# Half-block products for a first wave, a third half-block group for the second, and one written order for both

## The chip, the cores and the metric

The kernel runs on one core of a Trainium2 chip. The metric is the device time of one execution in microseconds (us). The core's engines are TensorE (PE in the profile, its weight loads PEld), VectorE (DVE), ScalarE (ACT), GpSimd (POOL) and SyncE (SP, which here issues most DMAs). Each works through its own queue in order and waits on semaphores for the others.

## The reference, cut to what matters

Block-wise linear attention with a decay `lam` for each head, over 4 batches, 8 heads, 768 positions of 64 values, in blocks of 64 with a carried state; then a two-layer MLP on the 3072 tokens of 512 values, with a quick gelu and a hidden width of 2048:

```python
for b in range(nb):
    intra = np.einsum('bhic,bhjc->bhij', qb, kb) * Dmask[None]
    intra = np.einsum('bhij,bhjd->bhid', intra, vb)
    inter = np.einsum('bhid,bhde->bhie', qb * lam_pow[None], kv_state)
    out[:, :, sl] = intra + inter
    kv_state = lam_block[None, :, None, None] * kv_state + np.einsum('bhsd,bhse->bhde', kb_dec, vb)

h = x @ w_in                                # 3072x512 @ 512x2048
g = h * (1.0 / (1.0 + np.exp(-1.702 * h)))
return (g @ w_out).astype(np.float32)       # 3072x2048 @ 2048x512
```

The kernel computes in bf16 with f32 sums and writes f32.

## The kernel before

**Waves.** The 3072 tokens are worked through in six waves of 512. Waves 0 and 1 (`w < ND`) take the first 256 positions of two batches each, `c` naming the batch of the pair; waves 2 to 5 take 128 positions of all four batches. While TensorE does the MLP of one wave, the attention of the next is put between its products. All of it stands under a manual schedule: the order of the instructions in the source is the order in each engine's queue, and the framework adds the semaphores.

**Attention of waves 0 and 1.** `do_cast` multiplies k or q by powers of `lam` and casts to bf16 (line 202, four operations of 128x256 a tile, on VectorE or GpSimd, with two SBUF inputs). `turn_pe` transposes on TensorE and copies out of PSUM on ScalarE. `cast_v` casts v. `d_scores` makes the scores of two pairs of heads and masks them on VectorE (line 267). `d_one` and `d_state` make the state, `d_keep` copies it to SBUF on ScalarE, `d_even` and `d_inter` read that copy. `d_out` makes the output; `d_x` copies it to `xT`, the MLP's input, one half by ScalarE and one by ScalarE or VectorE. For waves 2 to 5 the casts (line 209, GpSimd, eight instructions a wave) are followed by DMA transposes; a one-element copy on GpSimd (`gate_pool`, line 655) holds these casts back until the last of the wave's `x_sums`.

**Products by parts of the sum.** Most of the MLP is done by a scheme that forms a 2x2 block product from seven block products in place of eight. Its operands are blocks and sums of blocks, made on VectorE: `in_sums(g)` for `w_in` (tiles `w_in_t`, line 519, per group `g` of four 128-column blocks), `x_sums(w)` for the tokens (`x_s`, line 528), `weight_sums(j)` for chunk `j` of `w_out` (`w_out_t`, line 426) and `g_sums` for the hidden layer (`g_s`, line 439). The products are numbered 1 to 7 and gathered in three PSUM banks: X takes 1, then 6, 5 and 3 on top of it, Q takes 2, V takes 7 and then 4. Results leave between them: 1, 6 and 7 are copied out as `part` (ScalarE, or VectorE where the step ends in `v`), 2, 5 and 4 are `part` plus the bank (VectorE, lines 551 and 483), 3 is the bank itself. So product 6 has to wait for the copy of 1, 5 for that of 6, 3 for the sum of 5, and 4 for the copy of 7.

**First MLP product.** `in_product(w, g, n, ...)` is product `n` of group `g` for 256 of the 512 tokens by two output blocks: 4 matmuls of 256 columns. `mlp1` (line 402) and `mlp1_half` (line 414) are the plain forms, with 512 and 256 columns; their results go through gelu on ScalarE to `g_sb`. In wave 0 everything is plain; in wave 1 two groups (`GR[1]` = 0 and 3) are done by parts and the eight other blocks by `mlp1_half`; from wave 2 on all four groups are done by parts.

**Second MLP product.** `product(w, n, ts)` does product `n` for a wave (line 459). Wave 0 alone uses the plain `mlp2` (line 571): four groups of 128 tokens, 16 matmuls of 512 columns each.

**The order.** For waves 0 and 1 the order comes from a list of products (`main`) with the other work hung in at fractional places (`side`); from wave 1's groups on it is the string `STEPS[w]`, read by `one_step`. There a letter `a` to `d` with a digit is product n of the first to the fourth group, the capital with a digit its gelu, `Pnt` product n of the second MLP product for token half t, `S`, `M`, `m`, `R` parts of the next wave's attention, `X` its `x_sums`, `gl` and `gh` the `g_sums`, `K`, `Q`, `k`, `q` casts, `G` the gate, and `+` a step of the next wave.

**PSUM.** Eight banks in two rings: `mm` with three and `a` with five (`acc`). A new tile takes a bank of its ring and waits for the last reader of what stood there.

**DMA.** `w_in` and `w_out` come on GpSimd's queue, the rest on SyncE's. The loads of wave 1 are issued behind a small DMA that waits for the second chunk of `w_out` (line 658).

Of the kernel before, what the change touches and what calls it, by code (L numbers as in the profile page):

```python
# [25 lines left out]
def kernel(  # L26
# [394 lines left out]
    def weight_sums(j):  # L421
        b = w_out_sb[j].rearrange("p (m two) (c d) -> p two c m d", two=2, c=2)
        t1, t2, t3, t4 = (t[:, j * CW // 2 : (j + 1) * CW // 2] for t in TS)
        for o, x, y in ((t1, b[:, 0, 1], b[:, 0, 0]), (t2, b[:, 1, 1], t1),
                        (t3, b[:, 1, 1], b[:, 0, 1]), (t4, b[:, 1, 0], t2)):
            nc.vector.tensor_tensor(o, x, y, op=SUB)  # L426
# [138 lines left out]

    def mlp2(w, g, j):
        if j == 0:
            o_ps[w, g] = acc("ps_out", shape=[P, d_model], tag="mm")
        ps_out = o_ps[w, g]
        for fc in range(j * CW, (j + 1) * CW):  # L570
            nc.tensor.matmul(ps_out, g_of[w][:, fc, g * P : (g + 1) * P], w_out_sb[j][:, fc % CW, :],  # L571
                             start=(fc == 0), stop=(fc == FFC - 1))
        if j == NCH - 1:
            o = op.tile([P, d_model], f32, tag="o", name="o_sb")
            nc.vector.tensor_copy(o, ps_out)
            r0 = g // 2 * S + (g % 2) * P

            def store():
                for a, rows in enumerate((A, Z)):
                    nc.sync.dma_start(out=out[r0 : r0 + P].rearrange("(s a) d -> s a d", a=2)[:, a, :], in_=o[rows])  # L580
            late.append(store)

    def mlp_items(w):
        if w < ND:
            items = [(mlp1_half, w, c, fc) for c in range(HF) for fc in ((0, 2), HALVES)[w] if w or c or fc]
            if w == 0:
                items += [(mlp1, w, fc) for fc in range(4, FFC)]
        if w == 0:
            items += [(mlp2, w, g, j) for j in range(NCH) for g in range(3)]
            return items + [(mlp2, w, 3, j) for j in range(NCH)]  # L590
        return items + [(one_step, w, s) for s in STEPS[w].split()]

    def one_step(w, s):
# [66 lines left out]
    with tc.manual_schedule():  # L660
# [51 lines left out]
        mlp1_half(0, 0, 0)  # L712
# [4 lines left out]
        def start(w, c):  # L717
            if c == 0:
                d_one(w, c)
                d_keep(w, c)  # L720
            for pp in range(2):
                d_scores(w, c, pp)
            d_even(w, c, ("mm", "a")[c])

        def end(w, c):
            oa, oz = d_out(w, c)
            t = acc("ps_kv", shape=[P, NP, D]) if w else states[w, c]
            if w == 0:
                nc.scalar.copy(seen, oz[:, 3, P - 1 : P])
            d_state(w, c, t, Z)  # L730
            if w == 0:
                d_inter(w, c, oz, 0, False)
            if w and c == 0:
                d_one(w, 1)
# [6 lines left out]
            if w and c == 0:  # L741
                d_keep(w, 1)

        def stores():
            while late:
                late.pop(0)()

        side, main = [(0, (end, 0, 1))], []
        for w in range(ND):
            n = len(main)  # L750
            main += mlp_items(w)
            e = len(main)
            x = w + 1
            if x < ND:
                for c, (k_at, q_at, v_at, k_turn, q_turn, s_at, e_at) in enumerate(
                        ((19, 20, 19, 24, 25.5, 27, 30), (26.5, 28, 28, 29, 30, 32, 34))):
                    side += [(n + k_at, (do_cast, x, c, "k", (nc.vector, nc.gpsimd)[c])),
                             (n + q_at, (do_cast, x, c, "q", nc.vector)),
                             (n + v_at, (cast_v, x, c, ((pool_copy, pool_copy), (act_copy, act_copy))[c])),
                             (n + k_turn, (turn_pe, x, c, "k", act_copy)),  # L760
                             (n + q_turn, (turn_pe, x, c, "q", act_copy)),
                             (n + s_at, (start, x, c)), (n + e_at, (end, x, c))]
            else:
                for c in range(HF):
                    for t, nm in ((n + (2.1, 4.1)[c], "k"), (n + (3, 5)[c], "q")):
                        side += [(t, (do_cast, x, c, nm, nc.gpsimd)), (t, (turn_dma, x, c, nm))]
                side += [(n + 5.4, (stores,)), (n + 5.5, (load, x, "v")), (n + X_AT, (x_sums, w)), (n + T_AT, (weight_sums, NCH - 1))]
            if w == 0:
                side += [(n + t, (in_sums, g)) for t, g in IN_SUMS_AT]
                side += [(n + 14, (weight_sums, j)) for j in range(NCH - 1)]  # L770
                side += [(n + 12, (load, w + 2, "kq")), (n + 27, (stores,))]
        side.sort(key=lambda x: x[0])
        for i, (f, *a) in enumerate(main):
            while side and side[0][0] <= i:
                _, (g, *b) = side.pop(0)
                g(*b)
            f(*a)
        for _, (g, *b) in side:
            g(*b)
# [33 lines left out]
```

## Time and profile before

| | us |
|---|---|
| median of three runs | 193.75 |
| lowest and highest | 193.71, 194.22 |
| span of the profiled execution, first to last instruction | 191.5 |

The profile gives no other time for its execution than the span. Its mean granted TensorE clock is 1.00. The stretches that the change touches, from the chain of waits and the timeline:

| from, us | what TensorE does |
|---|---|
| 17.79 | first MLP product of wave 0 |
| 30.94 | second product of wave 0 (line 571), with the attention of wave 1 between |
| 49.05 | plain halves of wave 1's first product (line 414), attention of its second batch between |
| 57.83 | wave 1's two groups by parts (line 543) |
| 63.98 | wave 1's second product (line 459), with wave 2's attention |
| 78.41 | wave 2's groups |

In a timeline a row has the start, the duration, engine, line, operation and what is written and read, with a count where equal instructions are merged. A row of busy times by stretch gives the length, the busy time of PE, PEld, DVE, ACT and POOL with their counts, the granted clock, the busy share of the DMA engines and GB/s.

### The profile page before, as it was taken

The page shows a single profiled execution, that of the slowest core. Times are in us where ns is not written, and L with a number is a line of the kernel's source. Part 1 is how long each engine was busy: PE and PEld are TensorE (multiplying, and loading weights), DVE is VectorE, ACT ScalarE, POOL GpSimd, SP SyncE. Part 2 cuts the span into 40 slices and gives each one's busy share as a digit, 9 for nine tenths or more (in the row PEclk, how much of TensorE's full clock was granted, in tenths as well). Part 3 has the DMA queues.
Part 4 walks back from the last instruction along what each step waited for, and adds up shares of the span by engine and source line. Part 5 has one row for each costly group of instructions (what it writes and reads, how often), then busy time and mean ns, then how long its engine had stood idle before and what let it go on. Part 6 is the DMA issues. An engine that isn't in the chain of part 4 may idle for free.

```text
span 191.5 us, 5438 instructions
## 1 busy us (share of the span) xinstructions
PE 185.6 (97%) x2249; PEld 147.2 (77%) x2249; DVE 151.7 (79%) x288; ACT 127.9 (67%) x238; POOL 50.7 (26%) x73
## 2 busy tenths in 40 slices
PE   7999999999999999999999999999999999999993
PEld 2567544456788888888888888888888888888882
DVE  1896674488799799869799979799789797889950
ACT  4967664056676986389878288877488876597711
POOL 5478200044591000195000294000393000000000
PEclk9999999999999999999999999999999999999999
DMA  5999999999979898786989655999376903300113
GB/s 143 321 260 189 196 204 207 307 302 278 234 194 172 185 248 195 187 207 150 207 188 245 209 142 132 233 232 262 107 142 141 212 0 111 113 0 3 53 56 110
DMA packets 89086, 33.90 MB, mean 177 GB/s; under 512 B 67430, under 2 KB 88422, under 8 KB 89062
## 3 DMA queue, kind: packets, MB, share of 16 engines
q1 hardware_dynamic: 84164, 28.84, 61.0%
q0 software_dynamic: 4896, 4.72, 14.6%
q8 instruction: 17, 0.28, 0.6%
q14 instruction: 7, 0.06, 0.1%
q10 hardware_dynamic: 2, 0.00, 0.0%
HBM read 27.26 MB, written 6.29 MB: 175 GB/s over the span
## 4 chain that ended last, share of the span: by engine, by line
PE 85%; DMA 6%; DVE 4%; SPq 2%; POOL 1%; issue 1%; ACT 0%; ACTq 0%; POOLq 0%
PE ps_X L459 19%; PE ps_hX L543 16%; PE ps_V L459 9%; PE ps_hV L543 8%; PE ps_out L571 7%; PE ps_h L402 5%; PE ps_Q L459 5%; PE ps_hQ L543 4%; DMA w_in<-in_moe_w_in_dram 3%; DMA kf<-in_k_dram 3%; PE ps_s L335 2%; PE ps_o L390 2%; PE ps_h L414 2%; DVE w_out_t L426 2%; SPq L84 2%; DVE sm L267 1%
## 5 line engine op out<-in xcount | busy, mean ns | idle before, releaser
L459 PEld LDWEIGHTS <-g_s 128*128 128x128 bf16 x320 | 30.9, 98 | 4.1
L562 ACT ACTIVATE g_sb<-h_sb 128x512 bf16<-128x512 f32 x54 | 32.7, 632 | 1.2 <-DVE h_sb L551 1.2
L543 PEld LDWEIGHTS <-w_in_t 128*128 128x128 bf16 x288 | 28.1, 98 | 3.6 <-issue 0.3
L221 ACT COPY part<-ps_hX 128x512 f32<-128x512 f32 x32 | 18.3, 587 | 11.7 <-PE ps_hX L543 11.7
L459 PEld LDWEIGHTS <-g_sb 128*128 128x128 bf16 x240 | 22.8, 98 | 3.4
L543 PEld LDWEIGHTS <-w_in 128*128 128x128 bf16 x216 | 21.1, 98 | 2.4
L543 PE MATMUL ps_hX<-x_s,w_in_t 128*128 128x256 bf16 x144 | 21.6, 272 | 0.0
L459 PE MATMUL ps_X<-w_out_t,g_s 128*128 128x256 bf16 x160 | 19.1, 273 | 0.0
L439 DVE TENSOR_TENSOR g_s<-g_sb 128x1024 bf16<-128x1024 bf16 x20 | 13.7, 687 | 5.8 <-ACT g_sb L562 5.6
L209 POOL TENSOR_TENSOR ks<-kf,k_pow 128x512 bf16<-128x512 f32 x16 | 16.6, 1063 | 2.6 <-PE ps_o L316 2.6
L209 POOL TENSOR_TENSOR qs<-qf,q_pow 128x512 bf16<-128x512 f32 x16 | 16.6, 1062 | 2.3 <-DMA qf<-in_q_dram 2.3
L655 POOL CAST behind_q<-x_s 1x1 f32<-1x1 bf16 x3 | 0.5, 175 | 62.3 <-DVE x_s L528 62.3
L218 DVE COPY part<-ps_hV 128x512 f32<-128x512 f32 x18 | 12.4, 688 | 3.2 <-PE ps_hV L543 3.2
L571 PE MATMUL ps_out<-w_out,g_sb 128*128 128x512 bf16 x64 | 14.8, 379 | 0.0
L551 DVE TENSOR_TENSOR h_sb<-part,ps_hX 128x512 f32<-128x512 f32 x18 | 12.3, 681 | 2.7 <-PE ps_hX L543 2.7
L551 DVE TENSOR_TENSOR h_sb<-part,ps_hV 128x512 f32<-128x512 f32 x18 | 12.3, 684 | 1.0 <-PE ps_hV L543 1.0
L221 ACT CAST v_sb<-vf 128x1024 bf16<-128x1024 f32 (+1 forms) x13 | 11.0, 884 | 1.9 <-DMA vf<-in_v_dram 1.9
L551 DVE TENSOR_TENSOR h_sb<-part,ps_hQ 128x512 f32<-128x512 f32 x18 | 12.2, 679 | 0.0
L344 ACT ACTIVATE sm<-ps_s,inv_pow 128x512 bf16<-128x512 f32 x16 | 10.2, 690 | 2.5 <-PE ps_s L335 2.5
L562 ACT ACTIVATE g_sb<-ps_hX 128x512 bf16<-128x512 f32 x18 | 10.6, 589 | 1.8 <-PE ps_hX L543 1.8
L414 PE MATMUL ps_h<-xT,w_in 128*128 128x256 bf16 x96 | 11.3, 273 | 0.1
L348 DVE SCALAR_TENSOR_TENSOR sm<-ps_s,inv_pow,mask 128x512 bf16<-128x512 f32 x16 | 11.2, 744 | 0.0
(112 smaller groups left out, 359.5 us busy)
## 6 DMA issues: line engine op xcount, KB each, us to landing
kf<-in_k_dram SPq DMA_DIRECT2D x10, 512.0 KB, 6.6
qf<-in_q_dram SPq DMA_DIRECT2D x10, 512.0 KB, 6.4
vf<-in_v_dram SPq DMA_DIRECT2D x10, 512.0 KB, 6.1
out_dram<-o_sb SPq DMA_DIRECT2D x24, 128.0 KB, 2.4
out_dram<-o_sb SPq DMA_DIRECT2D x12, 256.0 KB, 2.1
w_out<-in_moe_w_out_dram POOLq DMA_DIRECT2D x4, 512.0 KB, 13.8
kf<-in_k_dram SPq DMA_DIRECT2D x4, 256.0 KB, 3.1
qf<-in_q_dram SPq DMA_DIRECT2D x4, 256.0 KB, 4.9
```

The costliest lines, as they stand in the source:

```text
L209: eng.tensor_tensor(x.rearrange("p b (r i j d) -> p j (b r) i d", i=2, j=2, d=D)[:, j], f.rearrange("p h (a d) -> p (h a) d", a=2).rearran ...
L218: nc.vector.tensor_copy(out, in_)
L221: nc.scalar.copy(out, in_)
L344: nc.scalar.activation(sm, s, COPY, scale=inv_pow[:, n : n + 1])
L348: nc.vector.scalar_tensor_tensor(sm, s, inv_pow[:, n : n + 1], mask.to_broadcast([P, B, P]), op0=MUL, op1=MUL)
L414: nc.tensor.matmul(h[:, u, :], w_in_sb[j][:, kc, i * P : (i + 1) * P], xT[w][:, kc, cols], start=(kc == 0), stop=(kc == KC - 1))
L439: nc.vector.tensor_tensor(o, x, y, op=f)
L459: nc.tensor.matmul(bank[:, t], x[:, m, t * P : (t + 1) * P], y, start=(n in (1, 2, 7) and t == ts[0] * last and m == 0), stop=(m == FFC // ...
L543: nc.tensor.matmul(bank[:, u], z[:, kc], y[:, kc], start=(n in (1, 2, 7) and u + kc == 0), stop=(kc == 1), skip_group_check=True)
L551: nc.vector.tensor_tensor(h, h_part[w, g, {2: 1, 5: 7, 4: 6}[n]], bank, op=ADD)
L562: nc.scalar.activation(g_of[w][:, a : b + 1 : b - a, 256 * i : 256 * i + 256], bank, GELU)
L571: nc.tensor.matmul(ps_out, g_of[w][:, fc, g * P : (g + 1) * P], w_out_sb[j][:, fc % CW, :], start=(fc == 0), stop=(fc == FFC - 1))
```

## The change

Wave 0's second product is done by parts (`product0`, `leave0`): products 1, 2 and 7 begin on the chunks of `w_out` and `g` that are there, product 4 has a bank of its own, W. `g_sums` and `weight_sums` are made for it chunk by chunk. Wave 1 does three groups by parts (`GR[1]` = 1, 2, 3) and two pairs of blocks plain, (14, 15) and (4, 13); the first two products of its groups a and b come ahead of the second batch's attention output. The differences of group 0 (`in_sums(0)`) move from wave 0 to the start of wave 2, behind all of `STEPS[1]`. The lists `main` and `side` give way to one written order for both waves, in which casts, copies, transposes and stores have new places.

```diff
-    def mlp1_half(w, c, fc):
+    def mlp1_half(w, c, a, b):
...
-            j, i = w_in_of[fc + u]
+            j, i = w_in_of[(a, b)[u]]
...
-        nc.scalar.activation(g_of[w][:, fc : fc + 2, cols], h, GELU)
+        nc.scalar.activation(g_of[w][:, a : b + 1 : b - a, cols], h, GELU)
...
-    def weight_sums(j):
+    def weight_sums(j, which=(0, 1, 2, 3)):
...
+        for i in which:
+            o, x, y = ops[i]
             nc.vector.tensor_tensor(o, x, y, op=SUB)
...
+    BANK0 = {1: "X", 6: "X", 5: "X", 3: "X", 2: "Q", 7: "V", 4: "W"}
+
+    def product0(n, m0, m1):
+        if m0 == 0 and n in (1, 2, 7, 4):
+            blocks[0, BANK0[n]] = acc(f"ps_{BANK0[n]}", shape=[P, 2, 256], tag="a" if n == 4 else "mm")
+        bank = blocks[0, BANK0[n]]
+        raw = [[token_half(0, i, kh) for kh in range(2)] for i in range(2)]
+        x = {1: raw[0][0], 2: raw[0][1], 4: raw[1][1]}
+        x = x[n] if n in x else half_sum[0][{5: 0, 6: 1, 7: 2, 3: 3}[n]]
+        for t in range(2):
+            for m in range(m0, m1):
+                y = {1: (0, 0), 2: (1, 0), 3: (1, 1)}.get(n)
+                y = w_half(m, *y) if y else TS[{4: 3, 5: 0, 6: 1, 7: 2}[n]][:, m]
+                nc.tensor.matmul(bank[:, t], x[:, m, t * P : (t + 1) * P], y,
+                                 start=(n in (1, 2, 7, 4) and t == 0 and m == 0),
+                                 stop=(m == FFC // 2 - 1), skip_group_check=True)
+
+    def leave0(n):
+        bank = blocks[0, BANK0[n]]
+        if n in (1, 6, 7):
+            part[0, n] = op.tile([P, 2, 256], f32, tag="part", bufs=6, name="part")
+            nc.scalar.copy(part[0, n], bank)
+            if n == 6:
+                nc.gpsimd.tensor_tensor(part[0, 6], part[0, 6], part[0, 7], op=ADD)
+            return
+        o = op.tile([P, 2, 256], f32, tag="o", name="o_sb")
+        if n == 3:
+            nc.scalar.copy(o, bank)
+        else:
+            nc.vector.tensor_tensor(o, part[0, {2: 1, 5: 7, 4: 6}[n]], bank, op=ADD)
...
+        late.append(store)
+
-    GR = {w: (1, 2, 0, 3) if w > 1 else (0, 3) for w in range(1, NW)}
-    TAGS = {w: ("aQXV", "mXVQ", "aQXV", "aXVQ") if w > 1 else ("aQXV", "aXVQ") for w in range(1, NW)}
-    HALVES = (0, 2, 5, 7)
-    IN_SUMS_AT, X_AT, T_AT = ((5, 1), (6, 2), (7, 3), (10, 0)), 3.5, 2.5
+    GR = {w: (1, 2, 0, 3) if w > 1 else (1, 2, 3) for w in range(1, NW)}
+    TAGS = {w: ("aQXV", "mXVQ", "aQXV", "aXVQ") if w > 1 else ({"X": "mm", "Q": "mm", "V": "a"}, {"X": "mm", "Q": "mm", "V": "a"}, {"X": "a", "Q": "a", "V": "a"})
+            for w in range(1, NW)}
...
-        if n == 1:
+        if isinstance(tag, dict):
+            if n in (1, 2, 7):
+                c = CHAIN[n]
+                h_bank[w, g, c] = acc(f"ps_h{c}", shape=[P, 2, 256], tag=tag[c])
+        elif n == 1:
...
-        1: ("a1 a7v a2 a6 b1 b7v A2 a5 b2 b6 B2 a4 a3 b5 b4 A5 P10 A4 b3 gl3 B4 B5 P11 gh3 S0 S1 M0 P20 m1 "
+        1: ("a7 a6 b7v b6 a5 c1 A5 b5 a4 c7v B5 A4 b4 c2 a3 B4 c6 C2 b3 c5 c4 P10 C5 c3 C4 gl3 P11 gh3 S0 S1 M0 P20 m1 "
             "Lk gl1 P70 P71 gl2 P21 v0 gh12 S2 S3 M2 m3 v1 o P40 P41 P60 gl4 gh4 P61 R P50 P51 +a1 X +a2 P30 "
             "P31 "),
```

The written order, in place of `main` and `side` (`stores(n)` now issues the next n stores; `sums` is `g_sums` of wave 0 and `t_sums` is `weight_sums`, both in the order 3, 1, 2, 4):

```diff
+        end(0, 1)
+        for c, a in ((0, 2), (1, 0), (1, 2)):
+            mlp1_half(0, c, a, a + 1)
+        in_sums(1)
+        for fc in range(4, 8):
+            mlp1(0, fc)
+        in_sums(2)
+        in_sums(3)
+        for fc in range(8, 10):
+            mlp1(0, fc)
+        sums(0, 4)
+        t_sums(0)
+        for fc in range(10, 12):
+            mlp1(0, fc)
+        sums(4, 6)
+        t_sums(1)
+        for fc in range(12, 16):
+            mlp1(0, fc)
+        sums(6, 8)
+        t_sums(2)
+        load(2, "kq")
+        for m0, m1 in ((0, 4), (4, 6)):
+            for n in (1, 2, 7):
+                product0(n, m0, m1)
+        t_sums(3)
+        product0(4, 0, 4)
+        for n in (1, 2, 7):
+            product0(n, 6, 8)
+            if n != 2:
+                leave0(n)
+        do_cast(1, 0, "k", nc.vector)
+        leave0(2)
+        do_cast(1, 0, "q", nc.vector)
+        product0(6, 0, 8)
+        leave0(6)
+        cast_v(1, 0, (pool_copy, pool_copy))
+        do_cast(1, 1, "k", nc.gpsimd)
+        cast_v(1, 1, (pool_copy, pool_copy))
+        turn_pe(1, 0, "k")
+        product0(4, 4, 8)
+        leave0(4)
+        turn_pe(1, 0, "q")
+        product0(5, 0, 8)
+        leave0(5)
+        stores(3)
+        start(1, 0)
+        d_one(1, 0)
+        d_keep(1, 0)
+        d_even(1, 0, "mm")
+        product0(3, 0, 8)
+        leave0(3)
+        do_cast(1, 1, "q", nc.vector)
+        turn_pe(1, 1, "k")
+        end(1, 0)
+        turn_pe(1, 1, "q")
+        d_one(1, 1)
+        mlp1_half(1, 0, 14, 15)
+        d_keep(1, 1)
+        start(1, 1)
+        for c in range(HF):
+            for nm in "kq":
+                do_cast(2, c, nm, nc.gpsimd)
+                turn_dma(2, c, nm)
+        stores(1)
+        load(2, "v")
+        mlp1_half(1, 0, 4, 13)
+        d_even(1, 1)
+        for s in "a1 a2 b1 A2 b2 B2".split():
+            one_step(1, s)
+        end(1, 1)
+        for a, b in ((14, 15), (4, 13)):
+            mlp1_half(1, 1, a, b)
+        x_sums(1)
+        for s in STEPS[1].split():
+            one_step(1, s)
+        in_sums(0)
         for w in range(ND, NW):
             for s in STEPS[w].split():
                 one_step(w, s)
```

`start(w, c)` is now the two `d_scores` alone, and `end(1, 0)` no longer makes the next batch's `d_one` and `d_keep`.

More of the change, by code (lines that the diff above doesn't have):

```diff
@@ new lines, in leave0, with store @@
+    def leave0(n):
[11 more added lines that the diff above has]
+            nc.vector.tensor_tensor(o, part[0, {2: 1, 5: 7, 4: 6}[n]], bank, op=ADD)
+        i, c = {2: (0, 0), 3: (0, 1), 4: (1, 0), 5: (1, 1)}[n]
+        def store():
+            rows5 = out.rearrange("(b t s a) d -> a b s t d", t=S // P, s=64, a=2)
+            for a, rows in enumerate((A, Z)):
+                nc.sync.dma_start(out=rows5[a, i, :, 0:2, 256 * c : 256 * c + 256], in_=o[rows])
+        late.append(store)
@@ L564 @@
     late = []
[L566 to L591, printed above, removed]
     def one_step(w, s):
@@ L711 @@
         d_scores(0, 1, 1, True)
-        mlp1_half(0, 0, 0)
+        mlp1_half(0, 0, 0, 1)
         d_one(0, 1)
@@ L717, in start @@
         def start(w, c):
-            if c == 0:
-                d_one(w, c)
-                d_keep(w, c)
             for pp in range(2):
                 d_scores(w, c, pp)
-            d_even(w, c, ("mm", "a")[c])
         def end(w, c):
@@ L732, in end @@
                 d_inter(w, c, oz, 0, False)
-            if w and c == 0:
-                d_one(w, 1)
             d_x(w, c, 0, oa, act_copy)
@@ L740, in end, with stores @@
                 nc.scalar.copy(kv_sb[0][:, 2 * w + c], t)
[L741 to L745, printed above, removed]
+        def stores(n):
+            for _ in range(n):
                 late.pop(0)()
[L748 to L779, printed above, removed]
+        def sums(m0, m1):
+            g_sums(0, m0, m1, (2, 0, 1, 3))
+        def t_sums(j):
+            weight_sums(j, (2, 0, 1, 3))
+        end(0, 1)
+        for c, a in ((0, 2), (1, 0), (1, 2)):
+            mlp1_half(0, c, a, a + 1)
```

4 lines of the change are left out of this document (2 added, 2 removed).

## The prediction

> **What bounds the kernel now.** I read the page's busy shares and its chain first, then the chain in order of time, then the busy times by stretch, and last VectorE and GpSimd instruction by instruction where they run at once.
>
> ```profile
> PE 185.6 (97%) x2249; PEld 147.2 (77%) x2249; DVE 151.7 (79%) x288; ACT 127.9 (67%) x238; POOL 50.7 (26%) x73
> PE 85%; DMA 6%; DVE 4%; SPq 2%; POOL 1%; issue 1%; ACT 0%; ACTq 0%; POOLq 0%
> 30.94 7.77 PE ps_out L571 x36
> 65.29 0.87 PE ps_X L459 x8
> 30.94:49.85 18.91, 18.91 (x225) 10.44 (x222) 13.25 (x30) 7.58 (x13) 5.54 (x8) 1.00 1.11 276
> 49.85:58.58 8.73, 8.58 (x150) 7.36 (x149) 8.23 (x11) 5.96 (x12) 6.80 (x6) 1.00 0.87 207
> 58.58:66.16 7.58, 7.58 (x70) 6.59 (x71) 6.77 (x12) 5.71 (x12) 0.00 (x0) 1.00 0.94 169
> 78.41:86.00 7.59, 7.59 (x71) 6.74 (x70) 5.99 (x12) 4.54 (x9) 5.21 (x7) 1.00 0.90 219
> ```
>
> TensorE is 85% of the chain and idle for 0.15 us in the four stretches that the change touches. Every matmul removed there is a gain, and every new wait of TensorE a loss of the same size. The chain gives the prices: 36 matmuls of 512 columns in 7.77 us, 0.216 each, and 8 of 256 columns in 0.87, 0.109 each. VectorE is nearly full in the second stretch (8.23 of 8.73).
>
> The next view decides most. GpSimd (POOL) and VectorE (DVE), one instruction a line (start, duration):
>
> ```profile
> 11.06 0.61 POOL L202 TENSOR_TENSOR ks<-kf,kd_pow 128x256 bf16<-128x256 f32 x1
> 11.32 0.62 DVE L202 TENSOR_TENSOR qs<-qf,qd_pow 128x256 bf16<-128x256 f32 x1
> 53.45 1.23 POOL L209 TENSOR_TENSOR ks<-kf,k_pow 128x512 bf16<-128x512 f32 x1
> 53.81 1.15 DVE L426 TENSOR_TENSOR w_out_t<-w_out,w_out_t 128x512 bf16<-128x512 bf16 x1
> 54.64 1.23 POOL L209 TENSOR_TENSOR ks<-kf,k_pow 128x512 bf16<-128x512 f32 x1
> 54.88 1.27 DVE L426 TENSOR_TENSOR w_out_t<-w_out 128x512 bf16<-128x512 bf16 x1
> 25.66 0.28 DVE L519 TENSOR_TENSOR w_in_t<-w_in 128x256 bf16<-128x256 bf16 x1
> 80.64 0.68 DVE L551 TENSOR_TENSOR h_sb<-part,ps_hQ 128x512 f32<-128x512 f32 x1
> 80.93 4.05 POOL L209 TENSOR_TENSOR ks<-kf,k_pow 128x512 bf16<-128x512 f32 x4
> 81.57 0.69 DVE L218 COPY part<-ps_hV 128x512 f32<-128x512 f32 x1 [0.25 <-PE ps_hV L543]
> 84.95 4.06 POOL L209 TENSOR_TENSOR qs<-qf,q_pow 128x512 bf16<-128x512 f32 x4
> ```
>
> A VectorE operation with two SBUF inputs ends 0.27 to 0.28 us after the GpSimd instruction under way: 11.06 + 0.61 = 11.67, and 11.32 + 0.62 = 11.94; 54.68 and 54.96; 55.87 and 56.15. One such operation gets through per GpSimd instruction, every 1.19 us. Those with a PSUM input (L551, L218) keep 0.68.
>
> **Removed work.** First wave: 64 x 0.216 = 13.8 us become 7 x 16 = 112 matmuls at 0.109, 12.2: 1.6 less. Second wave: 8 half products of 8 matmuls and two groups of 28 become 4 and three: 32 go, 28 come, 0.44 less. Together 2.0 us, all on the chain.
>
> **Added waits, first wave.** I carry the new order forward on the old clock, by the waits in the built program and by rows: 0.42 us for a 128x512 difference, the next start 0.34 later (0.46 if it reads the last), 0.6 between operations on PSUM, 0.59 for a ScalarE copy, 0.26 from a product's last matmul to its reader. The twelve half sums of `g_s` cost some 6 us of VectorE from 24.8 on, where `in_sums(0)` (25.13 to 27.08) is gone, and are hidden under the first product. TensorE starts the products at 30.94 as before. The third chunk's `w_out_t3` is ready at 34.6, when product 7 wanted it at 34.4: 0.2 lost. The last weight chunk, issued at 19.3, lands 16.6 later at 35.9, just in time. TensorE stands at `turn_pe(1,0,"q")` at 40.35. Its cast now stands behind four more difference operations and the sum for product 2 on VectorE: it ends at 40.9, 0.5 late. But in the same microseconds GpSimd now adds product 7 to 6 and then copies v, and L202 has two SBUF inputs: two of its four operations each wait out one GpSimd instruction (the add is not in the trace; nearest row 1.05 for 128x512, bounds 0.6 to 2.1). I take 42.2, 1.8 late. `d_even(1,0)` follows `d_keep` at once where the scores used to lie between: one ScalarE copy, 0.37, and its latencies, 0.5 lost. The cast of `turn_pe(1,1,"q")` ran from 45.36 to 46.8, just ahead of GpSimd's casts at 47.13; delayed to 47.5 it meets them, and ends at 50.3 instead of 49. The scores of the second pair, at 49.85 before, start at 49.4 without these meetings and at 52.0 with them: 2.6 between the two.
>
> **Added waits, second wave**, each told on the clock without the 2.6. `b2` takes the bank of `a2` and so waits for VectorE's sum, which now stands behind four masks: from 52.25 to 53.03, 0.8. `end(1,1)` is followed at once by half products that read its `xT`, and on ScalarE that copy stands behind the gelu of `b2`: TensorE is ready at 54.5, the copies end at 55.95, 1.55 lost. Before, 40 matmuls (4.4 us, the first of them of the other half) covered it. Two banks of the three are held by open products, so the second of these halves waits for the first one's gelu, 0.8. In the groups `c5` waits for a ScalarE copy behind five gelus, 1.0. Product 1 of the output then ends at 68.8, against 66.16: 2.6 late with the removed work counted, 5.2 with the first wave's meetings.
>
> **Moved: `in_sums(0)`.** Eight 128x256 differences now stand on VectorE after the sum at 80.64, so from 81.25, ahead of the copy of product `a7` (81.57). Behind that copy wait `a4`, then through the sum of `a5` also `a3`. GpSimd's gate has just been passed, and its eight instructions run from 80.93 to 89.0. Uncontended the eight cost 1.95 (25.13 to 27.08): the copy ends at 83.9, `a4` (84.15) is on time and `a3` 0.7 late. With one operation per GpSimd instruction, at 1.1 us a turn (1.01 and the turn), the last ends at 81.95 + 0.15 + 7 x 1.1 = 89.8, the copy at 90.45, `a4` starts 6.4 late, and `a3`, after one more copy and a sum, 7.1. An operation of this size beside GpSimd is not in the trace, so the bounds are 0.7 and 7.9 (1.19 a turn). I take 7.1, because the 11.32 row, also of 256 elements, ended by the same rule as those of 512. [...]
>
> **The sum:** -2.0 is inside the 5.2; 5.2 + 7.1 = 12.3. The profile gives 191.5 as its execution's span and no other time for it; so 203.8 as a span. The median of the runs, 193.75, lies 2.25 above it, and with that outside the span unchanged the forecast is 206.0, its own range 203 to 208.5 (the add, the turns, half a microsecond on the second wave's waits).
>
> **Rivals.** First, the meetings cost little: GpSimd starts later, or yields. Then 2.6 + 0.7 = 3.3, or 197.0, and up to 202 where only one of the two places is hit. For it: before has no 256-element bf16 difference beside GpSimd; against it the equal 0.27. Second, on the other side: TensorE's queue decides alone, because the new order gives VectorE and ScalarE their lead back wherever I see them late; 2.0 less, 191.7. It decides if all new waits together stay under 2.0. For it: from 18 to 188 us TensorE loses almost nothing although VectorE is 79% busy. Against it: `xT` and `b2` alone are 2.35, and no other matmul can pass them in the queue. Third, waits and gain cancel, 193.75. Fourth, the long wait has a price behind it: at the start the fills of 512 columns came 0.43 apart until about 6.7, then ran at the full rate; if an idle of 6.4 us brings that back for 5.3, half of it is lost, 2.7 more, 208.7. [...]
>
> **Chances.** Forecast 0.42, long wait with slow matmuls 0.12, cheap meetings 0.28, full gain 0.13, cancelling 0.05. The range runs from 195 to 209.5: what it leaves out is the last two. About 0.3% can be told from no change here, so faster is 0.13, same 0.05, slower 0.82.
>
> **What would show it.** Right: the eight differences at some 1.1 us each with GpSimd's casts beside them, and TensorE idle some 6 us ahead of `a4`; the cast L202 broken up near 40; an idle of 1.5 ahead of the halves after `end(1,1)`. Wrong: differences of 0.28 in a row there, or TensorE busy through 50 to 60.

## The result and the profile after

| us | before | after |
|---|---|---|
| median | 193.73 (4 runs, 193.13 to 194.22) | 207.51 (4 runs, 205.48 to 208.78) |
| span of the profiled execution | 191.5 | 203.8 |

The ratio is 1.068, 95% interval 1.0598 to 1.0762: slower. Ratios, here and below, leave out executions that took over 1.5% more than the quickest of the same kernel (here the 208.78; without it the median is 206.81), while medians and ranges count them all. The profiled execution is the quickest of the four after the change.

The page's busy shares, granted clock and chain for the changed kernel:

```profile
PE 187.9 (92%) x2293; PEld 153.4 (75%) x2293; DVE 162.8 (80%) x302; ACT 130.6 (64%) x243; POOL 53.4 (26%) x76
...
PEclk9999999999999999995899999999999999999999
...
PE 69%; DVE 13%; DMA 11%; ACT 3%; POOL 2%; issue 1%; SPq 1%; DVEq 0%; ACTq 0%
```

TensorE is busy 187.9 us instead of 185.6, although matmul work was taken out, and 69% of the chain instead of 85%. Two slices of the clock row, at some 92 to 102 us, are under full speed; before, none in this region was. The chain's pieces at product 1 of the output, for waves 1 and 2:

```profile
68.79 0.87 PE ps_X L461 x8
...
104.27 0.87 PE ps_X L461 x8
```

Before, the first of them began at 65.29, and the second is this row:

```profile
92.02 0.87 PE ps_X L459 x8
```

So 3.50 us are lost by the first and 12.25 by the second, and 12.3 at the end of the span: all of the loss lies ahead of 104 us, 3.50 in what the prediction calls the first and second wave (wave 0's second product, and wave 1), 8.75 at the start of wave 2. Where TensorE stood still before that, in its timeline (the bracket is the idle time and who ended it):

```profile
34.94 0.60 PE L510 MATMUL ps_V<-w_out_t,g_s 128*128 128x256 bf16 x4 [0.31 <-DVE w_out_t L428]
...
44.49 0.30 PE L298 MATMUL ps_o<-qT,kv 64*64 64x128 bf16 x4 [0.46 <-ACT kv L289]
...
53.64 0.60 PE L586 MATMUL ps_hQ<-xT,w_in 128*128 128x256 bf16 x4 [0.52 <-DVE h_sb L594]
...
56.71 1.03 PE L414 MATMUL ps_h<-xT,w_in 128*128 128x256 bf16 x8 [1.54 <-ACT xT L221]
...
58.43 1.03 PE L414 MATMUL ps_h<-xT,w_in 128*128 128x256 bf16 x8 [0.68 <-ACT g_sb L416]
...
66.45 0.60 PE L586 MATMUL ps_hX<-x_s,w_in_t 128*128 128x256 bf16 x4 [0.80 <-ACT part L221]
...
93.65 1.01 PE L586 MATMUL ps_hV<-xT,w_in_t 128*128 128x256 bf16 x4 [5.98 <-DVE part L218]
94.84 1.01 PE L586 MATMUL ps_hX<-x_s,w_in 128*128 128x256 bf16 x4 [0.18 <-DVE h_sb L594]
95.65 1.06 PE L586 MATMUL ps_hX<-xT,w_in 128*128 128x256 bf16 x4
96.50 1.06 PE L586 MATMUL ps_hX<-x_s,w_in_t 128*128 128x256 bf16 x4
```

Each of the forecast waits is there. A group of four matmuls is drawn 0.60 long (its end is modelled), but in an unbroken run the next starts 0.44 after it, so a wait costs 0.16 more than its bracket. After the wait of 5.98 the groups start 0.85 apart and not 0.44: the clock. Busy times by stretch, with the columns of before:

```profile
30.94:49.86 18.92, 18.09 (x275) 15.48 (x273) 16.06 (x38) 8.03 (x13) 7.44 (x10) 1.00 1.02 258
...
84.70:93.60 8.90, 2.97 (x28) 2.49 (x26) 8.83 (x11) 2.75 (x5) 8.15 (x8) 0.90 0.57 131
93.60:98.40 4.80, 4.57 (x21) 3.06 (x21) 3.07 (x5) 2.83 (x5) 0.00 (x0) 0.50 0.81 184
```

In the first stretch, wave 0's second product, TensorE is busy 18.09 us instead of 18.91, and the stretch is as long as before (18.92, 18.91): what the seven products save is idle time now. The waits of 0.31 and 0.46, at 0.16 more than the bracket each, take 1.1 of the 1.6 us that the prediction counted as saved there; the other 0.5 isn't assigned. In the second TensorE works 2.97 of 8.90 us while VectorE works 8.83 and GpSimd 8.15. In the third the granted clock is 0.50. What GpSimd and VectorE do in the second, from their timelines:

```profile
84.43 4.20 POOL L209 TENSOR_TENSOR ks<-kf,k_pow 128x512 bf16<-128x512 f32 x4
88.60 4.25 POOL L209 TENSOR_TENSOR qs<-qf,q_pow 128x512 bf16<-128x512 f32 x4
...
84.15 0.68 DVE L594 TENSOR_TENSOR h_sb<-part,ps_hQ 128x512 f32<-128x512 f32 x1
84.74 0.88 DVE L558 TENSOR_TENSOR w_in_t<-w_in,w_in 128x256 bf16<-128x256 bf16 x1
85.66 1.02 DVE L558 TENSOR_TENSOR w_in_t<-w_in,w_in_t 128x256 bf16<-128x256 bf16 x1
86.60 1.13 DVE L558 TENSOR_TENSOR w_in_t<-w_in 128x256 bf16<-128x256 bf16 x1
...
92.92 1.27 DVE L218 COPY part<-ps_hV 128x512 f32<-128x512 f32 x2
```

The differences of `in_sums(0)`, 0.28 each when they ran alone in wave 0, take 0.88 to 1.13 here, one for each GpSimd instruction, and the copy of `a7` that TensorE waits for stands behind all eight.

### The profile page after: what moved, and what is told of

It reads as the page before. It is cut to its first block, busy times and chain, and to the rows that moved or that the text cites. A ratio compares the mean times of both kernels' runs of the same rounds, so it can differ in the third digit from the quotient of the medians.

```text
span 203.8 us, 5556 instructions
## 1 busy us (share of the span) xinstructions
PE 187.9 (92%) x2293; PEld 153.4 (75%) x2293; DVE 162.8 (80%) x302; ACT 130.6 (64%) x243; POOL 53.4 (26%) x76
## 4 chain that ended last, share of the span: by engine, by line
PE 69%; DVE 13%; DMA 11%; ACT 3%; POOL 2%; issue 1%; SPq 1%; DVEq 0%; ACTq 0%
PE ps_X L461 17%; PE ps_hX L586 15%; PE ps_V L461 9%; PE ps_hV L586 8%; DMA w_out<-in_moe_w_out_dram 6%; PE ps_Q L461 4%; DVE w_in_t L558 4%; PE ps_hQ L586 4%; DMA vf<-in_v_dram 3%; DVE w_out_t L428 3%; DMA qf<-in_q_dram 2%; PE ps_s L335 2%; PE ps_o L390 2%; PE ps_h L414 2%; PE ps_X L510 2%; DVE g_s L441 2%
## 5 line engine op out<-in xcount | busy, mean ns | idle before, releaser
L605 ACT ACTIVATE g_sb<-h_sb 128x512 bf16<-128x512 f32 x57 | 34.7, 631 | 9.0 <-DVE h_sb L594 8.9
L586 PEld LDWEIGHTS <-w_in_t 128*128 128x128 bf16 x304 | 30.2, 99 | 11.2 <-issue 7.1
L586 PEld LDWEIGHTS <-w_in 128*128 128x128 bf16 x228 | 22.8, 100 | 4.3 <-issue 1.1
L586 PE MATMUL ps_hX<-x_s,w_in_t 128*128 128x256 bf16 x152 | 23.2, 276 | 0.8 <-ACT part L221 0.8
L441 DVE TENSOR_TENSOR g_s<-g_sb 128x1024 bf16<-128x1024 bf16 (+1 forms) x26 | 16.4, 645 | 5.9 <-ACT g_sb L605 5.9
L586 PE MATMUL ps_hV<-xT,w_in_t 128*128 128x256 bf16 x76 | 11.8, 280 | 6.0 <-DVE part L218 6.0
L218 DVE COPY part<-ps_hV 128x512 f32<-128x512 f32 x18 | 12.3, 686 | 3.5 <-PE ps_hV L586 3.4
L586 PE MATMUL ps_hQ<-xT,w_in 128*128 128x256 bf16 x76 | 11.6, 276 | 0.5 <-DVE h_sb L594 0.5
L586 PE MATMUL ps_hX<-x_s,w_in 128*128 128x256 bf16 x76 | 11.8, 280 | 0.2 <-DVE h_sb L594 0.2
L586 PE MATMUL ps_hX<-xT,w_in 128*128 128x256 bf16 x76 | 11.9, 280 | 0.0
L586 PE MATMUL ps_hV<-x_s,w_in_t 128*128 128x256 bf16 x76 | 11.9, 280 | 0.0
```

The source lines that it names most:

```text
L218: nc.vector.tensor_copy(out, in_)
L441: nc.vector.tensor_tensor(o, x, y, op=f)
L586: nc.tensor.matmul(bank[:, u], z[:, kc], y[:, kc], start=(n in (1, 2, 7) and u + kc == 0), stop=(kc == 1), skip_group_check=True)
L605: nc.scalar.activation(g_of[w][:, a : b + 1 : b - a, 256 * i : 256 * i + 256], bank, GELU)
```

## The experiments

Theory: the loss is (1) `in_sums(0)` taking turns with GpSimd's casts, (2) waits in the second wave that its new order opens, (3) matmuls at half clock after a long wait. Rivals: VectorE and GpSimd share by bytes and not by turns; GpSimd's casts are no part of it; the waits only move to the next tile. Ratios are each to runs of the kernel before on the same chip. Where the expectations have `in_sums(0)` or `in_sums(3)` at the start of the second wave, that is wave 2; GpSimd's casts for it are made partly during wave 1.

### e1_sums_early: the differences elsewhere

`in_sums` takes a list of the halves to make, and they stand apart in wave 1:

```diff
+        in_sums(0, (0,))      # after x_sums(1)
+        elif s[0] == "i":
+            in_sums(0, (int(a),))
-        1: ("... b4 c2 a3 B4 ...
+        1: ("... b4 c2 i1 a3 B4 ...
-        in_sums(0)            # ahead of wave 2
```

> The changed kernel, but in_sums(0) in two parts of four differences where VectorE and GpSimd both sit idle in wave 1: behind x_sums(1), and behind the sum of c2. Theory of turns (each of the eight differences waited out one GpSimd cast, and the clock fell behind the wait): 5.98 of waiting ahead of a4, 0.7 ahead of a3 and some 2 of slow matmuls go, the 3.5 lost before 69.5 stay; 193.73 + 3.5 = 197.2, 196.7 to 197.9. Rival (eight more differences load VectorE wherever they stand): 203 or more.

Measured: 200.00 (197.98 to 201.91), ratio 1.0264 (1.0135 to 1.0392). The eight differences take 0.28 to 0.29 each, and wave 2 starts without a wait and at full clock. Some 0.04 of the ratio's 0.068 is gone. But it came out 2 to 3 us above what was expected, and the profile shows why: the last cast of q in the first wave meets GpSimd, as it does not in the changed kernel's profiled execution. The timeline of VectorE, GpSimd and TensorE in e1:

```profile
47.89 3.33 DVE L202 TENSOR_TENSOR qs<-qf,qd_pow 128x256 bf16<-128x256 f32 x4
...
48.41 2.52 POOL L209 TENSOR_TENSOR ks<-kf,k_pow 128x512 bf16<-128x512 f32 x2 [0.19 <-DMA kf<-in_k_dram]
...
51.27 0.40 PE L238 MATMUL ps_t<-ident,qs 128*128 128x128 bf16 x4 [1.35 <-DVE qs L202]
```

Four operations that take 1.61 us alone (46.32, in the changed kernel) take 3.33: two of them take 1.26 each, beside one GpSimd cast each. TensorE waits 1.35 for them. Another 0.68 went to a chunk of `w_out` that landed late.

### e2_casts_held: the casts out of the way instead

```diff
-            gate_pool(x_sum[w][3][0:1, 0, 0:1])
+            gate_pool(TI[0][3][0:1, 0, 1, 0:1] if w == 2 else x_sum[w][3][0:1, 0, 0:1])
```

> The changed kernel with in_sums(0) in its place, but wave 2's GpSimd casts held until the last of the eight differences in place of the last x_sums. Theory of turns: the eight take 1.95 as they did in wave 0, the copy of a7 is late by some 2, a3 by 0.7; 197.9, 197.2 to 198.6. Rival (place and amount of VectorE's work, whatever GpSimd does): 205 to 207.

Measured: 198.61 (197.43 to 200.34), ratio 1.0234 (1.0121 to 1.0346). The differences stay where the change put them, GpSimd's casts wait until they are made, and they take 0.28 to 0.29 each. The first of the eight in VectorE's timeline, and what is left of the wait in TensorE's:

```profile
84.84 0.28 DVE L558 TENSOR_TENSOR w_in_t<-w_in,w_in 128x256 bf16<-128x256 bf16 x1
...
88.63 0.60 PE L586 MATMUL ps_hX<-x_s,w_in 128*128 128x256 bf16 x4 [0.43 <-DVE h_sb L594]
```

So it is not the place of the differences in VectorE's queue that costs the time, it is that they run beside GpSimd, whose casts start at 87.00 here. The forecast had `a3` 0.7 late without contention.

### e3_fills: the wait filled with matmuls

27 matmuls of 512 columns, whose results nothing reads, stand ahead of `a4` of wave 2, to keep TensorE at work through the wait.

```diff
+            for _ in range(int(a)):
+                nc.tensor.matmul(h_bank[w, GR[w][2], "X"], w_in_sb[0][:, 0, 0:P], w_in_sb[2][:, 0, :], start=True, stop=True)
...
-        2: ("... b2 b6 a4 A5 ...
+        2: ("... b2 b6 F27 a4 A5 ...
```

> The changed kernel with 27 matmuls of 512 columns on w_in, their result overwritten, in the wait ahead of a4 of wave 2 (27 x 0.216 = 5.8 us in a wait of 5.98). If the slow matmuls behind the wait come from the idle time: granted clock 1.00 throughout, some 2.1 less, 205.4, and less spread between runs. If they come from something else there: 207.5 as before.

Measured: 205.87 (205.09 to 208.08), ratio 1.0619 (1.05 to 1.0738). Against the changed kernel's 1.068 the medians alone settle nothing; the rows of TensorE's timeline do:

```profile
58.29 1.86 PE L414 MATMUL ps_h<-xT,w_in 128*128 128x256 bf16 x8 [1.54 <-ACT xT L221]
60.84 1.87 PE L414 MATMUL ps_h<-xT,w_in 128*128 128x256 bf16 x8 [0.69 <-ACT g_sb L416]
...
98.10 0.60 PE L588 MATMUL ps_hV<-xT,w_in_t 128*128 128x256 bf16 x4 [0.16 <-DVE part L218]
99.29 0.60 PE L588 MATMUL ps_hX<-x_s,w_in 128*128 128x256 bf16 x4 [0.59 <-DVE h_sb L596]
```

After the filled stretch the groups take 0.60 and not 1.01, so the slow matmuls of the changed kernel come from the idle time and not from the tiles they read. In this execution another stretch was slow: the groups of eight at 58.29 and 60.84, 1.86 instead of 1.03, with a granted clock of 0.51 from 58.2 to 63.0. It also waited 1.35 for the cast L202, as e1 did. The other three executions have a mean granted clock of 0.992 to 0.998, the changed kernel's four 0.975 to 0.983.

### e4a_again_8x256 and e4b_again_4x512: the turns by themselves

Both are the kernel before, with differences made once more, as extra work, just ahead of wave 2's steps: in e4a the eight of 128x256, in e4b four of 128x512, the same bytes in half the instructions.

```diff
+        in_sums(0)        # e4a
+        in_sums(3)        # e4b
```

> The kernel before, with in_sums(0) made once more (same values, eight differences of 128x256) at the start of wave 2, nothing else. Theory of turns: as in the changed kernel, 6.0 + 0.7 of waiting and 2 of slow matmuls, 202.5, 201.5 to 203.5. By bytes (0.6 a difference): 3.3, 197.0. Without contention: 194.5.

> The kernel before, with the four differences of in_sums(3) (128x512 each, four instead of eight of 128x256, the same bytes) made once more on VectorE at the start of the second wave, beside GpSimd's casts; extra work, the output is the same. By turns (one difference goes between two GpSimd operations, whatever its size): four turns of about 1.2 us, so a4 starts some 2.5 us late and a3 some 3.3 late, and the idle time is too short for the granted clock to fall: 196 to 198, 197.0. [...] With contention of no account: 194.5.

Measured: e4a 201.38 (200.79 to 202.4), ratio 1.0387 (1.0271 to 1.0502); e4b 198.56 (197.73 to 200.73), ratio 1.0225 (1.0123 to 1.0327). The timeline of VectorE in e4a, first and last of the eight and the copy behind them:

```profile
80.87 0.88 DVE L519 TENSOR_TENSOR w_in_t<-w_in,w_in 128x256 bf16<-128x256 bf16 x1
...
88.00 1.13 DVE L519 TENSOR_TENSOR w_in_t<-w_in,w_in_t 128x256 bf16<-128x256 bf16 x1
89.05 1.28 DVE L218 COPY part<-ps_hV 128x512 f32<-128x512 f32 x2
```

and in the timeline of e4b all four, with TensorE's wait:

```profile
81.81 1.01 DVE L519 TENSOR_TENSOR w_in_t<-w_in 128x512 bf16<-128x512 bf16 x1
82.85 1.15 DVE L519 TENSOR_TENSOR w_in_t<-w_in,w_in_t 128x512 bf16<-128x512 bf16 x1
83.93 1.27 DVE L519 TENSOR_TENSOR w_in_t<-w_in 128x512 bf16<-128x512 bf16 x1
85.12 1.26 DVE L519 TENSOR_TENSOR w_in_t<-w_in,w_in_t 128x512 bf16<-128x512 bf16 x1
...
87.03 0.60 PE L543 MATMUL ps_hV<-xT,w_in_t 128*128 128x256 bf16 x4 [2.31 <-DVE part L218]
88.23 0.71 PE L543 MATMUL ps_hX<-x_s,w_in 128*128 128x256 bf16 x4 [0.59 <-DVE h_sb L551]
88.74 1.06 PE L543 MATMUL ps_hX<-xT,w_in 128*128 128x256 bf16 x4
```

Eight take 8.2 us (80.87 to 89.05) and four of twice the size 4.5 (81.81 to 86.31): 1.02 and 1.12 each. By bytes the two would have taken as long as each other; here the number of instructions sets the time. (The 0.6 a difference of the rival by bytes is an estimate; it comes to half of the 1.15 to 1.27 that the prediction's rows show for 128x512 operations beside GpSimd.) This shows the turns, in a kernel that has nothing else of the change. e4b's expectation was wrong in one point: that the clock doesn't fall after so short a wait was the author's estimate, which no run had shown, and the row at 88.74 shows the fall; five groups from 88.23 to 92.07 took 3.84 us instead of 2.19. That is as much as the 1.6 us by which e4b was above 197.0.

### e5_wave2_order: the second wave's waits

e1_sums_early, and in the second wave the sum and output of the second batch stand ahead of `A2`, `b2`, `B2`, with one copy to `xT` on VectorE.

```diff
-        for s in "a1 a2 b1 A2 b2 B2".split():
+        for s in "a1 a2 b1".split():
             one_step(1, s)
         end(1, 1)
+        for s in "A2 b2 B2".split():
+            one_step(1, s)
...
-            mlp1_half(1, 1, a, b)
+            mlp1_half(1, 1, a, b, "a")
...
-            d_x(w, c, 1, oz, act_copy if w and c else dve_copy)
+            d_x(w, c, 1, oz, dve_copy)
...
-        1: ("... a3 B4 c6 C2 ...
+        1: ("... a3 c6 B4 C2 ...
```

> The changed kernel with in_sums(0) taken out of the start of the second wave as in e1_sums_early, and the start of the second wave's half-products put in another order: the end of the first group's sum and the second half-block's product go ahead of A2, b2 and B2, the oz copy of d_x on VectorE, c6 ahead of B4. By the theory that the 3.5 us late in product 1 of the output are waits for h_sb (0.52), xT (1.54), g_sb (0.68) and part (0.80): most of these go, 2 to 3 us less than e1_sums_early: 197 to 198. If the earlier sums of the second wave meet GpSimd's casts, up to 2.3 us of it come back later: 199.5. By a rival, that the waits only move to the next tile: as e1_sums_early, 200.

Measured: 195.69 (194.74 to 196.73, 10 runs), ratio 1.0114 (1.008 to 1.0148), below what was expected. Of the four waits 0.52, 1.54, 0.68 and 0.80 one of 0.29 is left in TensorE's timeline, and these two are longer:

```profile
48.92 0.40 PE L238 MATMUL ps_t<-ident,qs 128*128 128x128 bf16 x4 [1.26 <-DVE qs L202]
58.58 0.60 PE L586 MATMUL ps_hX<-x_s,w_in_t 128*128 128x256 bf16 x4 [0.89 <-DVE x_s L567]
```

The waits did not just move to the next tile. The sums of x come earlier now and meet GpSimd (0.89), and the cast L202 does so again (1.26).

### e6_casts_behind and e7_wave1_order: two more repairs

```diff
+        gate_pool(TI[0][3][0:1, 0, 0, 0:1])   # e6: behind in_sums(0, (0,)); ahead of the casts q of half 0, k and q of half 1
...
-        for m0, m1 in ((0, 4), (4, 6)):       # e7
-            for n in (1, 2, 7):
-                product0(n, m0, m1)
+        for n in (1, 2, 7):
+            product0(n, 0, 4)
+        for n in (1, 2):
+            product0(n, 4, 6)
         t_sums(3)
         product0(4, 0, 4)
+        product0(7, 4, 6)
...
-        leave0(2)
         do_cast(1, 0, "q", nc.vector)
+        leave0(2)
...
-        d_even(1, 0, "mm")
         product0(3, 0, 8)
+        d_even(1, 0, "mm")
```

> As e5_wave2_order, with three of GpSimd's four casts of the second wave's start held until VectorE's first in-sum is made, so that the sums there run alone. If meetings of VectorE with GpSimd cost e5_wave2_order anything, this takes it away: 194 to 196. If there is no meeting there: the same as e5_wave2_order within 0.5 us. If the held casts come late for the turn of q and k: slower, 199 or more.

> As e6_casts_behind, with the first wave's parts of the product in another order: the seventh product's last part goes behind the fourth, the leave of half-block 2 behind the cast of q, d_even behind the third product. By the theory that the first wave's waits (0.31, 0.24, 0.46) are open time of TensorE: about 1 us less than e6_casts_behind, 193 to 195, which would be no slower than the kernel before. By the rival, that the cast of L202 and GpSimd meet there now and then whatever the order: no gain, 194 to 196.

Measured: e6 198.17 (197.37 to 198.41), ratio 1.0223 (1.0155 to 1.029); e7 196.02 (195.71 to 196.48), ratio 1.0121 (1.0055 to 1.0187). Neither came down as expected. In e6 the sums of x run alone (0.42 each), and the wait for them is gone, but a slow stretch came behind the wait for qs (granted clock 0.75 from 53 to 58). In e7 the waits 0.31, 0.24 and 0.46 of the first wave are gone from TensorE's timeline, and these are there:

```profile
48.80 0.40 PE L238 MATMUL ps_t<-ident,qs 128*128 128x128 bf16 x4 [1.49 <-DVE qs L202]
...
69.47 0.51 PE L335 MATMUL ps_s<-qT,kT 64*128 64x128 bf16 x12 [1.59 <-DMA qT<-qs]
```

The casts that were held make the DMA transposes of q late: 1.59 paid for 0.89 saved.

### e8_meeting_gated, e9_all_repairs, e10_wave2_gate: one gate behind the last L202

```diff
+        gate_pool(cast[1, 1, "q"][0:1, 0, HD - 1 : HD])
         for c in range(HF):
             for nm in "kq":
                 do_cast(2, c, nm, nc.gpsimd)
```

e8 is the changed kernel with this gate alone, e9 is e7_wave1_order with it in place of the gate behind the in-sum, e10 is e5_wave2_order with it.

> The changed kernel, where GpSimd's casts for the second wave (L209) wait until VectorE's last cast of the first wave's second pair (L202) is made; nothing else. In the changed kernel's own profile the two did not meet; in four later profiles of kernels with the same first wave they did, and TensorE waited 1.26 to 1.49 us for qs. If the changed kernel meets them in most of its executions, its median (207.5, where its profiled execution took 205.5) holds the price: with the gate 205 to 206, and less spread. If the meeting there costs nothing, 207.5. If the gate makes GpSimd late for the second wave's turns: 208.5 or more.

> As e7_wave1_order, with GpSimd's four casts held behind the last L202 instead of behind the second wave's first in-sum. e7_wave1_order waited 1.49 for qs, 1.59 for a DMA of qT, 0.69 and 0.29, and its span was 194.8; the gate takes the 1.49 away and, being some 10 us earlier than the old one, the 1.59 too: span 191.5 to 192.5, median 193 to 194, about the kernel before. If the sums of x then meet the casts as in e5_wave2_order (0.89): 1 us more.

> As e5_wave2_order (span 193.3, median 195.7) with GpSimd's four casts held behind the last L202. The wait for qs (1.26) and the cast's 1.8 us on VectorE go: span 191.5 to 192.3, median 193.2 to 194.2. If the first wave's order in e7_wave1_order is worth its 0.5 to 1 us, e9_all_repairs is that much below this one; if not, they are the same.

Measured: e8 206.48 (203.8 to 207.61), ratio 1.0597 (1.0535 to 1.0659); e9 194.98 (193.86 to 197.35, 12 runs), ratio 1.0067 (1.0035 to 1.0099); e10 195.95 (194.39 to 197.05), ratio 1.0109 (1.0058 to 1.0159). In all three profiles no L202 on VectorE is longer than 0.62 and TensorE waits 0.24 at most for qs: the gate does what it should. Yet e8 and e10 came out above what was expected, and e9 at the value given for the case that the sums of x meet the casts. In e10's profile one sum of x makes TensorE wait 1.76. In e8's, at 207.61 its slowest execution, the clock falls a second time, behind the second wave's waits of 0.52 and 1.54, as in e3:

```profile
56.22 1.87 PE L414 MATMUL ps_h<-xT,w_in 128*128 128x256 bf16 x8 [1.54 <-ACT xT L221]
```

And e8 against 1.068 and e10 against e5 overlap in their intervals, so what the meeting costs the median isn't settled (207.51 and 206.48 differ by 1 us, 195.69 and 195.95 by nothing). e9 has the lowest ratio of the study and is still slower than the kernel before. Its timeline has one larger wait left, behind the sums of x:

```profile
56.14 1.15 DVE L567 TENSOR_TENSOR x_s<-x_s,xT 128x512 bf16<-128x512 bf16 x1
57.33 1.15 DVE L567 TENSOR_TENSOR x_s<-xT,x_s 128x512 bf16<-128x512 bf16 x1
...
57.35 0.60 PE L586 MATMUL ps_hX<-x_s,w_in_t 128*128 128x256 bf16 x4 [1.39 <-DVE x_s L567]
```

### e11_sums_clear: that meeting taken away too

```diff
-        for c in range(HF):
-            for nm in "kq":
-                do_cast(2, c, nm, nc.gpsimd)
-                turn_dma(2, c, nm)
+        for nm in "kq":
+            do_cast(2, 0, nm, nc.gpsimd)
+            turn_dma(2, 0, nm)
...
         x_sums(1)
-        in_sums(0, (0,))
+        gate_pool(x_sum[1][3][0:1, 0, 0:1])
+        for nm in "kq":
+            do_cast(2, 1, nm, nc.gpsimd)
+            turn_dma(2, 1, nm)
...
-        1: ("... c2 i1 a3 c6 ... C4 gl3 P11 ...
+        1: ("... c2 i0 a3 c6 ... C4 gl3 i1 P11 ...
```

> As e9_all_repairs (span 192.1, median 195.0), with GpSimd's casts of q and k for half 1 held behind the last of the second wave's sums of x, and the two halves of in_sums(0) put where GpSimd rests (after c2, and between the two sums of g). e9_all_repairs lost 1.39 to a sum of x that took turns with GpSimd (two sums of 1.15 us instead of 0.42, one of 1.27 instead of 0.4). By turns, this wait goes: span 190.7 to 191.2, median 193 to 194, within 0.5 us of the kernel before. If the spread of 2 to 3 us between executions comes from elsewhere (loads that land late), the median stays at 194 to 195. If the half-1 turns come late: slower, 196 or more.

Measured: 199.51 (198.03 to 200.89), ratio 1.032 (1.026 to 1.038): slower than the kernel before by 3.2%, and than e9 by 2.5%, as its last clause had it. The four sums of x take 0.42 to 0.43 and TensorE doesn't wait for them. But the turn of half 1 now stands on SyncE's queue behind two stores and two loads, and its DMAs are issued at 64.65 and 67.96 (59.69 and 61.02 in e9):

```profile
64.65 3.22 SPq L245 DMA_TRANSPOSE kT<-ks  x1
67.96 1.25 SPq L245 DMA_TRANSPOSE qT<-qs  x1
...
71.00 0.82 PE L335 MATMUL ps_s<-qT,kT 64*128 64x128 bf16 x12 [4.02 <-DMA qT<-qs]
```

The stretch behind it, 71.0 to 75.0, has a granted clock of 0.64. A meeting of 1.39 was taken away and a wait of 4.02 put in its place.

## Why the prediction was right, and where its terms were not

The sum, 12.3 on the span, is what the profiled execution shows (203.8 - 191.5). It is so by terms that made up for each other, so that it fits to a tenth is luck:

| part, us late | predicted | profiled execution |
|---|---|---|
| first wave's casts meet GpSimd | 2.6 | 0 |
| the rest up to product 1 of the output | 2.6 | 3.5 |
| turns of `in_sums(0)`, up to `a3` | 7.1 | 6.5 |
| matmuls at half clock behind it | 0 (a rival, 2.7) | 2.2 |
| sum | 12.3 | 12.2 |

**In-sums.** Right in mechanism, and e2, e4a and e4b show it by three ways. The size: `a4` lost 5.98 + 0.16 = 6.14 instead of 6.4, `a3` a further 0.34 (without what the clock took of its 0.75), because a turn took 1.05 and not 1.1: from the end of the first difference (85.62) to that of the last (92.99) seven turns took 7.37.

**The first wave's meetings** is the step that failed: in size, and at the first of its two places in mechanism too. It was forecast at 2.6 as a matter of course. At the first place, the turn of q near 40, the cast and GpSimd's add did run at once:

```profile
39.58 1.43 DVE L202 TENSOR_TENSOR qs<-qf,qd_pow 128x256 bf16<-128x256 f32 x4
...
40.17 1.96 POOL L520 TENSOR_TENSOR part<-part 128x512 f32<-128x512 f32 x1 [20.37 <-ACT part L518]
```

But it was the add that waited. The four casts took 0.42 each, as alone, and the add ended 1.12 after the last of them. VectorE's next operation then waits 1.16 for the add, and so it does in e1, e2 and e5 (in e1 and e2 the four casts take 1.42 and 1.43 in all); in e7, where the cast stands one place earlier on VectorE, the add took 1.27. TensorE lost 0.24 at most there, not 1.8. Why the two engines gave way the other way round here than at `in_sums(0)` isn't shown. At the second place the profiled execution had no meeting: the casts ran through at 46.32 (1.61), and GpSimd's came only at 48.90. The place was right: the meeting is in five of the six later profiles of kernels with this cast and no gate (e1, e3, e5, e6, e7), at 1.26 to 1.49 where 1.3 was forecast; in e2, where the four casts took 1.83, TensorE didn't wait. In e1 and e5 GpSimd's cast there started when a load landed (after 0.19 and 0.40 us of idle time), so it is a price that some executions pay and others don't.

**The second wave's waits.** 0.8, 1.55, 0.8 and 1.0 were forecast. The brackets with 0.16 each give 0.68, 1.70, 0.84 and 0.96, the same 4.2 in all. Of the 0.9 by which the sum of this part was short, 0.46 had gone by the scores of the second pair (49.86 instead of 49.4 without meetings). The rest lies in the prediction's addition: the terms that it names, 0.45 gained by the scores, 4.15 of waits and 0.44 of matmuls, give 3.3 and not 2.6. What runs the other way, some 0.2, is for the most part the 0.15 for which TensorE was idle there before. e5 shows that these waits came from the order: with another order of the same work its profile has 0.29 and 0.89 in their place. The ratio went from 1.0264 to 1.0114, with intervals that overlap a little.

**Slow matmuls** were held apart as a rival with 0.12 and a time of 208.7. They came, at 2.2 us (groups from 94.84 to 98.86 in 4.02 instead of 2.19, and 0.41 of `a4`), and e3 shows that the idle time brings them. Of the 6.8 us at half clock (91.82 to 98.64) some 1.8 lay within the wait itself. The forecast and this rival weren't alternatives; the rival's term belonged in the sum.

**Cheap meetings and full gain** are refuted by the differences' rows and by TensorE's 2.97 of 8.90. The first was half true: in the profiled execution only one of the two places was hit, for which up to 202 was given; by the prediction's own terms that case is 2.6 + 7.1 = 9.7, or 203.4, and it leaves out the slow matmuls and 0.9 of other waits.

**From span to median.** The 2.25 added for what lies outside the span was too much: in every run on record the time is 1.7 to 1.8 above the span (205.48 and 203.8 here). The medians, 207.51 against 206.0, differ by what the other three executions (206.81 to 208.78) have above the profiled one. Their mean granted clock was 0.975, that of the profiled one 0.983. A stretch of 3.41 us at half clock, half as long as the profiled one's 6.82, lowers the mean over 205 us by 0.008 (1.71 of 205), so by this estimate each had one such stretch more, worth up to 1.7 us. e8's profile has one of twice this length behind the second wave's waits; where it lay in these three, and what else they waited for, wasn't profiled.

**The saved work** is real, and idle: 18.09 busy of 18.92. With the order repaired (e9) the kernel is 0.67% slower than before (0.35 to 0.99%), so even then the gain of 2.0 wasn't cashed in.

## What to carry to other kernels

Before moving work on VectorE, look at what GpSimd does in the same microseconds: where GpSimd is at a row of instructions, a small operation with two SBUF inputs can take as long as one of them (in e4a 1.02 us for 128x256, in e4b 1.12 for 128x512, against 0.28 and 0.42 alone), so make few and large ones there, or put them where GpSimd rests. A wait's price is its length and the slow matmuls that can follow (6.14 and 2.2 us in the changed kernel); add both to the sum. Holding back GpSimd's casts is only free as long as the DMA transposes behind them, and their place in the issuing queue, aren't late (TensorE waited 1.59 for one in e7, 4.02 in e11).

## What the runs showed of the hardware

**Turns.** Beside GpSimd, 128x256 differences took 1.02 and 128x512 ones 1.12 us apiece, 0.28 and 0.42 alone. With the same bytes, eight instructions took 8.2 us (e4a) and four took 4.5 (e4b). The four casts L202 near 40 kept 0.42 each in a row while GpSimd's add had begun, and the add ended 1.12 after them: there GpSimd was the one that waited.

**The clock.** In these traces the granted clock falls to 0.50 for some 3.4 or 6.8 us at a time: in the changed kernel from 91.82 to 98.64, in e3 from 58.3 to 65.1, in e8 from 56.2 to 63.0 and once more from 93.7, in e4b from 88.6 to 92.0, in e6 from 52.0 to 55.5, in e11 from 70.4 to 73.9, and in e4a for some 6.8 us up to 93.2 (all but the first worked out from the granted clocks of stretches and of the span and from TensorE's rows). The falls have no fixed place beside a wait: the changed kernel's comes 4.1 us into its wait of 5.98, those of e3 and the first of e8 at about the end of the wait of 1.54, e4b's some 1.5 us after the end of its wait of 2.31, with one of 0.59 between.

It takes no single long wait, and the same waits do it in one execution and not in another. In the 3.4 us ahead of the fall, as long as the shorter of these stretches, TensorE was idle throughout in the changed kernel, for 2.5 in e4b, for 1.9 in e3 and e8 (a part of the wait of 0.52 and the whole or nearly the whole of the 1.54) and for 1.34 in e6. In the changed kernel itself the waits of 1.54 and 0.68 put 2.2 us of idle time into the 3.4 up to 58.43, and the clock stayed at 1.00 (57 to 63); in e10 0.24 and 1.76 make 2.0 in the 3.4 up to 60.45, and it stayed at 1.00 too (58 to 65). So these runs give no threshold, and what sets the moment of a fall isn't shown.
